# The last segment's keys and values are computed with the tokens moving, and the attention steps get another order

## The chip, the cores and the metric

The kernel runs on one core of one Trainium2 chip. The metric is the device time of one execution in microseconds (us). Three runs of the kernel before took 2739.06, 2739.63 and 2742.57 us; their median is 2739.63 us.

## The reference, cut to what matters

One transformer block on 2048 tokens of width 1024: a modulated layer norm, attention with a memory over 32 heads of 32, an output projection, a second modulated norm, and a gated feed-forward network. The tokens are four segments of 512. The part that the change touches:

```
h = layernorm(x) * (1 + ca) + sa
q, k, v = h @ wq, h @ wk, h @ wv            # 32 heads of 32
for s in range(4):                          # segments of 512 tokens
    logits = qs @ ks.T * scale + mask       # mask as in the reference
    a_dot  = softmax(logits) @ vs
    a_mem  = (phi(qs) @ M) / (phi(qs) @ z + 1e-6)
    o      = g * a_mem + (1 - g) * a_dot    # g = sigmoid(beta)
    M, z   = M + phi(ks).T @ vs, z + sum(phi(ks))
x = x + ga * (o @ wo)
```

After the last segment M and z are not needed any more, so of its keys only ks in the logits is used.

## The kernel before, in words

Everything is float32. Products run on TensorE (PE) in its fp32r form. For accuracy an operand is split into a high and a low part, and a product is three matmuls: high by high, low by high, high by low.

**Steps.** Eight groups of four heads times four segments make 32 steps. Steps 0 to 15 take segments 0 and 1 of each group in turn, steps 16 to 31 segments 2 and 3; so the last segment is that of the odd steps from 17 on. The loop in `attention` runs n from 0 to 32. In its round n it computes the scores of step n, the values of step n - 1 and the projections of step n + 1, all interleaved. The projections for the last segment are therefore made in the even rounds 16 to 30.

**What sets the order.** No scheduler works here: the instructions of all five engines stand in the order in which the code issues them, and that is written by hand in the table ORDER, a string of short names for every round. The names that matter:

- K0 to K7 (K in round 0): the products of keys and values in eight pieces, `keys` in `project_in` (L384). The hidden tokens (128 of them) are the operand held in the array, the weights of keys and values (256 columns) move past. A piece is 12 matmuls. Q0 to Q3: the queries' product, six matmuls a piece (L390), weights held and 512 tokens moving.
- o0, o1: ScalarE (ACT) copies the keys and VectorE (DVE) the values out of PSUM (L401, L402). kt: TensorE turns the keys (four transposes, L418), ACT and DVE split them (L421, L422). dk, dq: DMAs that spread keys and queries over the rows of `ks` and `qs`.
- qo, ea, eb: split and exponent of the queries (L447 to L461).
- S0 to S3: the scores of 128 queries by 128 to 512 keys, four heads (L541), their row maxima on DVE (L543) and exponents with row sums on ACT (L545). tr: the logarithm of the row sums (L550). tm, tq: maxima and logarithms are joined, turned and written into `qs` on DVE (L554 to L565). T needs them.
- T0 to T3: the scores once more, transposed (L629), exponent on ACT (L631), the triangle cut on GpSimd (POOL, L632). P0, P2: their product with the values (L641). rm, yt, zs: the memory's part is added and the result stored.
- A, mz, nu, dn: the memory's state (L580) and its numerators and denominators.
- G, C and D, l, L and m: load of the next group's weights, their high part on ACT (L369), their low part on POOL (L375). wl, wd: columns of the modulation. x: the hidden tokens of segments 2 and 3 are loaded and split. In rounds 31 and 32 all K and Q stand for pieces of the output projection (L708) instead, six matmuls each; every piece also runs a step of side work, such as `load_late`, which multiplies the second half of `wo` by the gate (DVE, L685) and splits it (ACT L189, POOL L194).

**Buffers.** Two PSUM banks take the products of K and Q in turn, five take S, T and all small results, one the output of P. A bank is used again when its readers are done.

After the attention come the rest of the output projection and the feed-forward network, two stages with 4704 and 2352 matmuls (L1133, L1347), which the change leaves as they are.

Of the kernel before, what the change touches and what calls it, by code (L numbers as in the profile page):

```python
# [12 lines left out]
F32R = mybir.dt.float32r  # L13
AF = mybir.ActivationFunctionType
# [14 lines left out]
NSEG = 4  # L29
# [7 lines left out]
def block_kernel(ctx: ExitStack, tc: tile.TileContext, x, c, wmod, wq, wkv, wo, beta, wg, wu, wd, out):  # L37
    nc = tc.nc
    f32 = lambda ap: ap.bitcast(F32)
# [53 lines left out]
    def mm_ps(name):  # L93
        return psum.tile([P, L], F32, name=name, tag="mm", bufs=2)
# [4 lines left out]
    def s_ps(name):  # L99
        return small[0].tile([P, L], F32, name=name, tag="s", bufs=small[2])  # L100
# [9 lines left out]
    def t2(name, tag, bufs=1, dt=F32, shape=(P, L)):  # L110
        return (p1 if tag in ("qs", "row") else pa).tile(list(shape), dt, name=name, tag=tag, bufs=bufs)
# [241 lines left out]
    ks_t = []  # L353
# [32 lines left out]
    def q_mm(ps, g, s, kt, **kw):  # L386
        hi, lo = hT[s][kt]
        w = W[g][0].rearrange("p h (k m) -> p h k m", m=P)[:, :, kt]
        for a, b in ((0, hi), (0, lo), (1, hi)):
            nc.tensor.matmul(ps, w[:, a], b, start=(kt == 0 and a == 0 and b is hi), stop=(kt == KT - 1 and a == 1), **kw)  # L390
# [421 lines left out]
    def feed_forward():  # L812
# [562 lines left out]
        for m in range(NCH):  # L1375
# [32 lines left out]
    steps = [(hf, g, s) for hf in range(2) for g in range(G) for s in (2 * hf, 2 * hf + 1)]  # L1408
    ORDER = {
        (0,):  # L1410
            "N K K N G1 K N N G2 K G0 K S0 S1 C1 S2 K S3 C2 K l1 l2 A tr tm tq L1 K K L2 K",
        (1,):
            "T0 K0 mz K1 T1 A P0 T2 ns K2 K3 nc D0 T3 n0 K4 nd n1 o0 K5 S0 m0 Q0 S1 K6 S2 m1 Q1 S3 Q2 Q3 nu dn ne nl K7 "
            "qo tr P2 o1 rm ea tm tq kt dq dk yt eb zs ek",
        (2, 4, 6, 8):
            "wd Q0 G2 Q1 Q2 T0 ns Q3 T1 P0 nc T2 A T3 qo n0 K0 nd S0 K1 ea C2 S1 G1 eb dq K2 S2 K3 C1 n1 l2 K4 l1 S3 K5 "
            "P2 nl o0 L2 tr tm K6 tq rm L1 K7 yt G0 wl o1 kt dk ek zs ne",
        (3, 5, 7):
            "mz D0 K0 K1 m0 T0 K2 T1 K3 ns m1 P0 nc T2 wl o0 n0 Q0 S0 K4 A S1 Q1 S2 K5 S3 n1 Q2 K6 nl Q3 tr wd T3 tm qo "
# [12 lines left out]
            "K5 C1 S3 x ea A wd l1 L1 G0 eb K6 dq x K7 P2 o1 tr rm tm kt tq yt ek x dk x x zs x x",
        (15,):
            "D0 K0 m0 K1 m1 K2 T0 K3 o0 T1 K4 S0 Q0 S1 Q1 S2 mz Q2 x S3 A tr Q3 P0 x T2 tm K5 T3 nu K6 K7 wl tq qo ea P2 "
            "o1 x eb wl rm dn x wd kt dq yt dk zs ek",
        (16,):
            "K0 G1 wd T0 mz x Q0 T1 A P0 x T2 Q1 T3 G2 Q2 S0 K1 S1 Q3 S2 K2 K3 o0 qo ea C2 C1 S3 tr P2 l2 G0 rm l1 eb K4 "
            "K5 K6 tm dq K7 o1 nu tq yt L2 dn kt L1 ek dk zs",
        (17,):
            "K0 D0 m0 K1 m1 K2 T0 K3 T1 P0 T2 o0 Q0 T3 wl S0 S1 Q1 S2 Q2 Q3 qo S3 K4 K5 ea K6 K7 P2 mz eb o1 tr rm tm kt "  # L1440
            "tq dq yt dk nu dn ek zs",
        (18, 20, 22, 24, 26, 28):
            "K0 G2 K1 K2 T0 mz K3 G1 o0 T1 K4 S0 C2 Q0 S1 P0 S2 Q1 T2 G0 Q2 Q3 wd T3 qo C1 K5 S3 K6 l1 A K7 P2 o1 tr dq "
            "tm kt L1 rm yt wl ek tq l2 nu dn dk ea eb L2 zs",
        (19, 21, 23, 25, 27):
            "K0 D0 K1 K2 m0 T0 K3 o0 wl T1 K4 S0 Q0 S1 P0 mz m1 wd wd T2 wl Q1 T3 S2 Q2 Q3 qo K5 S3 K6 dq K7 P2 o1 tr tm "
            "kt tq rm yt nu dk dn ek zs ea eb",
        (29,):
            "K0 D0 K1 m0 wd K2 T0 K3 o0 ga T1 K4 S0 K5 wo mz S1 P0 S2 m1 Q0 ga S3 Q1 tr wo tm Q2 T2 Q3 T3 K6 P2 K7 qo ea "
            "nu tq rm dq o1 yt dn kt eb dk ek wl zs",  # L1450
        (30,):
            "mz K0 ga x x T0 K1 T1 wp wp K2 K3 wl wl P0 o0 S0 K4 S1 Q0 S2 Q1 x wo x S3 x wo x Q2 K5 tr x K6 T2 K7 T3 wp "
            "Q3 tm tq nu qo P2 x ea o1 dq eb rm yt dn A x kt dk x x x x zs ek",
# [119 lines left out]
    def attention(nseg1):  # L1573
# [145 lines left out]
```

## Time and profile before

| what | value |
|---|---|
| median of three runs | 2739.63 us |
| the profiled execution's own time | 2743.34 us |
| its span, first to last instruction | 2741.5 us |
| granted TensorE clock, mean | 0.998 |
| busy: PE / DVE / ACT / POOL | 2706.3 / 1545.3 / 1191.4 / 843.6 us |
| attention, rounds 0 to 32 | up to about 980 us |
| scores' first matmuls of rounds 18 and 30 begin at | 573.10 and 903.50 us |

The views are read as follows. A row of a group has its line, engine and operation, what is written and read, the shape and the count; then its busy time, the mean length of one in ns, and the idle time of the engine just before it with what ended it. Matmuls overlap in their pipeline, so the mean length of one is longer than the distance from one to the next; that is the busy time of a long unbroken run by its count. A row of waits has the waiting instruction, what ended the wait, the sum in us, how often, and the longest. A row of a stretch has its borders and length, then for each engine busy time and count, the granted TensorE clock, the share of the DMA engines and GB/s. A row of the timeline has start, length, engine, line, operation, and in brackets the idle time before it.

### The profile page before, as it was taken

The page shows a single profiled execution, that of the slowest core. Times are in us where ns is not written, and L with a number is a line of the kernel's source. Part 1 is how long each engine was busy: PE and PEld are TensorE (multiplying, and loading weights), DVE is VectorE, ACT ScalarE, POOL GpSimd, SP SyncE. Part 2 cuts the span into 40 slices and gives each one's busy share as a digit, 9 for nine tenths or more (in the row PEclk, how much of TensorE's full clock was granted, in tenths as well). Part 3 has the DMA queues.
Part 4 walks back from the last instruction along what each step waited for, and adds up shares of the span by engine and source line. Part 5 has one row for each costly group of instructions (what it writes and reads, how often), then busy time and mean ns, then how long its engine had stood idle before and what let it go on. Part 6 is the DMA issues. An engine that isn't in the chain of part 4 may idle for free.

```text
span 2741.5 us, 42690 instructions
## 1 busy us (share of the span) xinstructions
PE 2706.3 (99%) x14620; PEld 2270.8 (83%) x14620; DVE 1545.3 (56%) x3455; ACT 1191.4 (43%) x2811; POOL 843.6 (31%) x1446
## 2 busy tenths in 40 slices
PE   7999999999999999999999999999999999999999
PEld 6888888888888878888888888888888888888887
DVE  7676666667667735555555555343443254575456
ACT  6777777676767624333323233111111033233323
POOL 4333234423333534254455452443531000000000
PEclk9999999999999999999999999999999999999999
DMA  7455444444443558778898778999998687795563
GB/s 261 110 153 142 121 142 143 131 112 139 119 133 104 166 197 294 250 287 328 307 356 308 266 278 278 358 364 356 359 358 313 218 316 254 263 305 200 184 206 125
DMA packets 244889, 637.76 MB, mean 233 GB/s; under 512 B 24768, under 2 KB 49344, under 8 KB 244672
## 3 DMA queue, kind: packets, MB, share of 16 engines
q1 hardware_dynamic: 244672, 635.03, 68.5%
q8 instruction: 116, 1.90, 0.3%
q14 instruction: 101, 0.83, 0.1%
HBM read 372.79 MB, written 211.81 MB: 213 GB/s over the span
## 4 chain that ended last, share of the span: by engine, by line
PE 91%; DVE 3%; DMA 2%; ACT 1%; issue 1%; POOL 1%; SPq 0%; DVEq 0%; ACTq 0%; POOLq 0%
PE f L1133 38%; PE y L1347 19%; PE kv L384 11%; PE q L390 6%; PE y L708 5%; PE S L541 3%; PE T L629 3%; PE O L641 3%; DVE qs L565 1%; ACT sj L545 1%; PE M L580 1%; PE kv L513 1%; PE num L597 1%; PE tpb L267 0%; PE kT L418 0%
## 5 line engine op out<-in xcount | busy, mean ns | idle before, releaser
L1133 PE MATMUL f<-A,B 128*128 128x512 f32 x4704 | 1072.9, 390 | 0.1
L1133 PEld LDWEIGHTS f<-A,B 128*128 128x128 f32 x4704 | 881.6, 188 | 184.4 <-issue 1.0
L1347 PE MATMUL y<-B,L 128*128 128x512 f32 x2352 | 533.3, 389 | 0.0
L1347 PEld LDWEIGHTS y<-B,L 128*128 128x128 f32 x2352 | 441.6, 188 | 91.5
L545 ACT ACTIVATE sj<-sj,mm 128x384 f32<-128x384 f32 (+3 forms) x512 | 281.8, 556 | 59.3 <-DVE mm L543 57.8
L543 DVE CUSTOM_DVE_ANT_0 sj<-S,mask 128x384 f32<-128x384 f32 (+3 forms) x512 | 226.0, 488 | 90.4 <-PE S L541 65.7
L632 POOL TENSOR_SCALAR_AFFINE_SELECT pt<-pt 128x128 f32<-128x128 f32 x512 | 161.8, 335 | 366.2 <-ACT pt L631 359.1
L631 ACT ACTIVATE pt<-T 128x256 f32<-128x256 f32 (+3 forms) x512 | 181.9, 441 | 141.1 <-PE T L629 136.8
L847 ACT ACTIVATE L<-X 128x512 fp32r<-128x512 f32 x168 | 105.8, 629 | 259.1 <-PE y L1347 166.9
L384 PE MATMUL kv<-w,hhh 128*128 128x256 f32 x1024 | 200.0, 285 | 0.0
L849 DVE TENSOR_TENSOR L<-X,L 128x512 fp32r<-128x512 f32 x168 | 116.0, 691 | 147.1 <-ACT L L847 147.1
L1167 ACT ACTIVATE g<-g 128x512 f32<-128x512 f32 x56 | 35.4, 631 | 369.4 <-DVE g L1166 369.4
L384 PE MATMUL kv<-w,hha 128*128 128x256 f32 x896 | 178.1, 286 | 0.3 <-DVE vx L402 0.3
L1072 POOL TENSOR_TENSOR rw<-rw,gbb 128x256 f32<-128x256 f32 x112 | 92.2, 858 | 249.3 <-DMA rw<-wd 184.8
L384 PEld LDWEIGHTS kv<-w,hhh 128*128 128x128 f32 x1024 | 164.8, 190 | 1.5 <-issue 0.4
L375 POOL TENSOR_TENSOR w<-r,w 128x256 fp32r<-128x256 f32 x180 | 131.5, 760 | 98.6 <-ACT w L369 98.6
L384 PEld LDWEIGHTS kv<-w,hha 128*128 128x128 f32 x896 | 145.7, 191 | 2.4 <-issue 0.8
L384 PE MATMUL kv<-w,hlh 128*128 128x256 f32 x512 | 144.6, 282 | 0.0
L708 PE MATMUL y<-wo,hho 128*128 128x512 f32 x384 | 127.3, 396 | 0.8 <-DVE xr L712 0.6
L384 PE MATMUL kv<-w,hla 128*128 128x256 f32 x448 | 126.8, 283 | 0.0
L1154 ACT ACTIVATE g<-f 128x512 f32<-128x512 f32 x56 | 33.5, 598 | 204.4 <-PE f L1133 204.4
L629 PE MATMUL T<-qs,ks 128*128 128x256 f32 (+3 forms) x512 | 108.0, 330 | 6.4 <-DVE qs L565 4.4
(240 smaller groups left out, 4093.0 us busy)
## 6 DMA issues: line engine op xcount, KB each, us to landing
bc_d<-B SPq DMA_DIRECT2D x189, 512.0 KB, 5.2
B<-bc_d SPq DMA_DIRECT2D x189, 512.0 KB, 5.6
B<-wc_d SPq DMA_DIRECT2D x112, 512.0 KB, 4.1
hid_d<-g SPq DMA_DIRECT2D x56, 512.0 KB, 4.3
wc_d<-T SPq DMA_DIRECT2D x56, 512.0 KB, 7.2
X<-hid_d SPq DMA_DIRECT2D x112, 256.0 KB, 4.7
wr<-gd_d SPq DMA_DIRECT2D x84, 256.0 KB, 4.1
qs<-qh SPq DMA_DIRECT2D x64, 256.0 KB, 3.6
```

The lines of the kernel that those rows point to most:

```text
L375: nc.gpsimd.tensor_sub(w[:, 1, c], r[:, c], f32(w[:, 0, c]))
L384: nc.tensor.matmul(ps, b[:, sl], w[:, a], start=(kt == 0 and a == 0 and b is hi), stop=(kt == KT - 1 and a == 1), **kw)
L390: nc.tensor.matmul(ps, w[:, a], b, start=(kt == 0 and a == 0 and b is hi), stop=(kt == KT - 1 and a == 1), **kw)
L543: nc.vector.tensor_tensor_reduce(out=sj[:, :nv], in0=ps[:, :nv], in1=mask[:, L - nv:], scale=-1.0, scalar=3.4e38, op0=ALU.add, op1=ALU.min ...
L545: nc.scalar.activation(sj[:, :nv], sj[:, :nv], AF.Exp, bias=mm[:, j, i:i + 1], scale=-1.0, accum_out=ll[:, i, j:j + 1])
L629: nc.tensor.matmul(ps[:, :nn], ks[:, j, kc * P:(kc + 1) * P], qs[:, j, L - nn:], start=True, stop=True)
L631: nc.scalar.activation(pt, ps[:, nn - n:nn], AF.Exp)
L632: nc.gpsimd.affine_select(pt[:, :P], pt[:, :P], pattern=[[1, P]], compare_op=ALU.is_ge, fill=0.0, base=0, channel_multiplier=-1)
L708: nc.tensor.matmul(ps, b[:, i * P:(i + 1) * P], w[:, a, g % 2], start=(g == 0 and a == 0 and b is hi), stop=(g == G - 1 and a == 1))
L849: eng.tensor_sub(lo[:, k], src[:, k], f32(hi)[:, k])
L1133: nc.tensor.matmul(ps, B[m, i][:, a, kt * P:(kt + 1) * P], A[p, i, kt][b], start=(start and kt == 0 and a == 0 and b == 0), stop=(kt == 3 ...
L1347: nc.tensor.matmul(banks[t], ops[k][:, y, t * P:(t + 1) * P], B[slots[k]][:, x], start=(i not in (2, 4, 3) and j == 0 and x == 0 and y == ...
```

## The change

For the last segment `project_last` takes the place of `project_in`. Its K0 to K3 make the keys and K4 to K7 the values, with the weights held and 512 tokens moving: six matmuls of 512 columns in a piece instead of twelve of 256. Keys come out turned already, so o0 splits them at once (ACT and DVE); values come out with tokens in the columns, o1 copies them (ACT), and a new name vt turns them (four transposes, one DVE copy) in place of kt.

```diff
+    def side_mm(ps, g, s, half, kts):
+        for kt in kts:
+            hi, lo = hT[s][kt]
+            w = W[g][1 + kt // 4].rearrange("p h (k m) -> p h k m", m=2 * P)[:, :, kt % 4, half * P:(half + 1) * P]
+            for a, b in ((0, hi), (0, lo), (1, hi)):
+                nc.tensor.matmul(ps, w[:, a], b, start=(kt == 0 and a == 0 and b is hi), stop=(kt == KT - 1 and a == 1))
+
+    def project_last(u, n, g, s):
...
+        def columns(i):
+            half, q = divmod(i, 4)
+            if q == 0:
+                ps[half] = mm_ps(f"{'kv'[half]}T{nm}")
+            side_mm(ps[half], g, s, half, (2 * q, 2 * q + 1))
...
+        def keys():
...
+            nc.scalar.activation(t["h"], ps[0], AF.Copy)
+            nc.vector.tensor_sub(t["l"], ps[0], f32(t["h"]))
+
+        def vals():
+            t["v"] = t2("vt" + nm, "kn")
+            nc.scalar.activation(t["v"], ps[1], AF.Copy)
+
+        def turned():
...
+            vs = s_ps("vv" + nm)
+            for i in range(4):
+                nc.tensor.transpose(vs[:, i * P:(i + 1) * P], t["v"][:, i * P:(i + 1) * P], ident)
+            nc.vector.tensor_copy(vx[:, :, :P], vs.rearrange("p (t m) -> p t m", m=P))
...
-                project_in(u, n + 1, *steps[n + 1][1:])
+                (project_last if steps[n + 1][2] == NSEG - 1 else project_in)(u, n + 1, *steps[n + 1][1:])
```

All strings of ORDER are new. Two of them, of the last round and of the even rounds from 18 to 28:

```diff
         (18, 20, 22, 24, 26, 28):
-            "K0 G2 K1 K2 T0 mz K3 G1 o0 T1 K4 S0 C2 Q0 S1 P0 S2 Q1 T2 G0 Q2 Q3 wd T3 qo C1 K5 S3 K6 l1 A K7 P2 o1 tr dq "
-            "tm kt L1 rm yt wl ek tq l2 nu dn dk ea eb L2 zs",
+            "G2 K0 wl K1 T0 wd K2 T1 K3 o0 P0 mz T2 A G1 T3 G0 S0 K4 S1 C1 P2 S2 dk K5 Q0 S3 tr Q1 Q2 C2 tm l1 Q3 K6 tq "
+            "qo rm L1 K7 l2 nu o1 yt dn ea eb dq L2 zs vt",
         (32,):
-            "K0 Q0 K1 K2 T0 Q1 T1 K3 Q2 P0 T2 Q3 T3 K4 K5 K6 P2 rm yt zs K7",
+            "Q0 K0 K1 K2 T0 K3 T1 Q1 P0 T2 Q2 T3 K4 P2 K5 rm K6 K7 yt zs Q3",
```

Three places at which the engines' rows differ. Changed lines have numbers higher by 55 from L541 on (L545 is L600, L550 is L605, L629 is L684, L631 is L686).

*PE, first product for the last segment (round 16).* `kv_3` is the PSUM tile of keys and values, `kT_3` that of the turned keys, `hhh` and `hlh` are high and low parts of the hidden tokens, `w_1` the weights. Before:

```order
L418 MATMUL kT_2_7157<-ident,kn_2_6777 128x128 x4
L384 MATMUL kv_3_0_7181<-w_1_0_6635,hhh_1_0_6751 128x256
L384 MATMUL kv_3_0_7181<-w_1_0_6635,hlh_1_0_6752 128x256
L384 MATMUL kv_3_0_7181<-w_1_0_6635,hhh_1_0_6751 128x256
L384 MATMUL kv_3_0_7181<-w_1_0_6635,hhh_1_1_6758 128x256
...
L629 MATMUL T_1_00_7197<-qs_1_6617,ks_117 128x512
```

Now:

```order
L418 MATMUL kT_2_7158<-ident,kn_2_6764 128x128 x4
L503 MATMUL kT_3_7190<-hhh_1_0_6758,w_1_0_6546 128x512
L503 MATMUL kT_3_7190<-hlh_1_0_6759,w_1_0_6546 128x512
L503 MATMUL kT_3_7190<-hhh_1_0_6758,w_1_0_6546 128x512
L503 MATMUL kT_3_7190<-hhh_1_1_6826,w_1_0_6546 128x512
...
L684 MATMUL T_1_00_7203<-qs_1_6535,ks_117 128x512
```

Between the same neighbours twelve matmuls of 256 columns have become six of 512 (the rows left out go on in the same way), held and moving operand have changed places, and the tile holds keys alone.

*ACT and PE, from round 0 to round 1.* `sj` are exponents of scores, `w_0_1` high parts of the next group's weights, `ln` the logarithm of the row sums, `kn` copies of keys. ACT before, and now:

```order
L545 ACTIVATE sj_0_23_896,ll_0_806<-sj_0_23_896,mm_0_805 128x512
L545 ACTIVATE sj_0_33_901,ll_0_806<-sj_0_33_901,mm_0_805 128x512
L369 ACTIVATE w_0_1_904<-r_0_1_771 128x1024
L550 ACTIVATE ln_0_932<-ll_0_806 128x16
L401 ACTIVATE kn_1_690<-kv_1_0_693 128x256
L401 ACTIVATE kn_1_690<-kv_1_1_694 128x256
L421 ACTIVATE kh_1_975<-kT_1_970 128x512
L447 ACTIVATE qh_1_979<-q_1_695 128x512
```

```order
L600 ACTIVATE sj_0_23_892,ll_0_802<-sj_0_23_892,mm_0_801 128x512
L600 ACTIVATE sj_0_33_897,ll_0_802<-sj_0_33_897,mm_0_801 128x512
L605 ACTIVATE ln_0_900<-ll_0_802 128x16
L369 ACTIVATE w_0_1_902<-r_0_1_823 128x1024
L369 ACTIVATE w_0_1_928<-r_0_1_769 128x1024
L401 ACTIVATE kn_1_690<-kv_1_0_693 128x256
L401 ACTIVATE kn_1_690<-kv_1_1_694 128x256
L421 ACTIVATE kh_1_973<-kT_1_968 128x512
```

The logarithm has moved ahead of the split of the weights, and both splits (the first stood between the second and third row of scores) now follow it. PE at the same border; `kT` are the turned keys of step 1, `kv_0` the first products of round 1, `T` the transposed scores. Before, and now:

```order
L418 MATMUL kT_1_970<-ident,kn_1_690 128x128 x4
L629 MATMUL T_0_00_1000<-qs_0_601,ks_116 128x512
...
L629 MATMUL T_0_30_1015<-qs_0_601,ks_116 128x512
L384 MATMUL kv_0_0_1023<-w_0_1_847,hha_0_263 128x256
L384 MATMUL kv_0_0_1023<-w_0_1_847,hla_0_264 128x256
```

```order
L418 MATMUL kT_1_968<-ident,kn_1_690 128x128 x4
L384 MATMUL kv_0_0_1005<-w_0_1_928,hha_0_263 128x256
...
L384 MATMUL kv_0_0_1005<-w_0_1_902,hha_7_534 128x256
L684 MATMUL T_0_00_1065<-qs_0_601,ks_116 128x512
...
L684 MATMUL T_0_30_1080<-qs_0_601,ks_116 128x512
L267 MATMUL tpa_0_1085<-ident,na_676 128x128 x4
```

T0 came right behind the turned keys; now four pieces, K0 to K3 with 48 matmuls (rows left out), stand between them.

*ACT, end of round 32.* `pt` are the exponents of T2 (`pt_3_32` is its last) and T3 (`pt_3_03` on), `wo` and `ks` the second half of the output weights, whose split waits for the gate's product. Before, and now:

```order
L631 ACTIVATE pt_3_32_13704<-T_3_32_13702 128x256
L189 ACTIVATE wo_1_13715<-ro_0_13676 128x1024
L631 ACTIVATE pt_3_03_13724<-T_3_03_13722 128x128
L631 ACTIVATE pt_3_13_13729<-T_3_13_13727 128x128
L631 ACTIVATE pt_3_23_13734<-T_3_23_13732 128x128
L631 ACTIVATE pt_3_33_13739<-T_3_33_13737 128x128
L189 ACTIVATE wo_2_13750<-ro_1_13713 128x1024
L189 ACTIVATE ks_116<-ro_2_13748 128x1024
L189 ACTIVATE ks_117<-ro_3_13764 128x1024
```

```order
L686 ACTIVATE pt_3_32_13293<-T_3_32_13291 128x256
L686 ACTIVATE pt_3_03_13309<-T_3_03_13307 128x128
L686 ACTIVATE pt_3_13_13314<-T_3_13_13312 128x128
L686 ACTIVATE pt_3_23_13319<-T_3_23_13317 128x128
L686 ACTIVATE pt_3_33_13324<-T_3_33_13322 128x128
L189 ACTIVATE wo_1_13335<-ro_0_13305 128x1024
L189 ACTIVATE wo_2_13358<-ro_1_13333 128x1024
```

The split of `wo_1` stood ahead of T3's exponents, now it stands behind them. POOL, which follows the same order, has T3's four cuts ahead of the low parts of `wo_1` likewise.

More of the change, by code (lines that the diff above doesn't have):

```diff
@@ L495, in project_in, with queries @@
         after_kv(u, n, s, nm, lambda: st)
+        after_q(u, n, s, nm, lambda: ps["q"])
+    def side_mm(ps, g, s, half, kts):
[5 more added lines that the diff above has]
+    def project_last(u, n, g, s):
+        nm = f"{g}_{s}"
+        ps, t = {}, {}
+        ks = ks_t[n % 2]
+        ST[n] = [None, ks, None, None]
+        def columns(i):
[3 more added lines that the diff above has]
+            side_mm(ps[half], g, s, half, (2 * q, 2 * q + 1))
+        def queries(i):
+            if i == 0:
+                ps["q"] = mm_ps("q" + nm)
+            for kt in (2 * i, 2 * i + 1):
+                q_mm(ps["q"], g, s, kt)
+        def keys():
+            t["h"] = t2("kh" + nm, "sp", bufs=4, dt=F32R)
+            t["l"] = t2("kl" + nm, "sp", bufs=4, dt=F32R)
+            nc.scalar.activation(t["h"], ps[0], AF.Copy)
[4 more added lines that the diff above has]
+        def turned():
+            vx = t2("vx" + nm, "vx", bufs=3, shape=(P, 4, P + 2))
+            nc.gpsimd.memset(vx[:, :, P:], 1.0)
+            ST[n][2] = vx
+            vs = s_ps("vv" + nm)
+            for i in range(4):
+                nc.tensor.transpose(vs[:, i * P:(i + 1) * P], t["v"][:, i * P:(i + 1) * P], ident)
+            nc.vector.tensor_copy(vx[:, :, :P], vs.rearrange("p (t m) -> p t m", m=P))
+        for i in range(8):
+            u[f"K{i}"] = lambda i=i: columns(i)
+        for i in range(4):
+            u[f"Q{i}"] = lambda i=i: queries(i)
+        u["o0"] = keys
+        u["o1"] = vals
+        u["vt"] = turned
+        u["dk"] = lambda: spread(ks, ((0, t["h"]), (1, t["h"]), (2, t["l"])))
         after_q(u, n, s, nm, lambda: ps["q"])
@@ L1438, in block_kernel @@
[L1438 removed]
+            "G1 K0 K1 T0 K2 T1 P0 T2 mz K3 o0 T3 K4 G2 S0 K5 S1 P2 C2 C1 rm S2 Q0 K6 S3 Q1 l1 tr Q2 yt nu dn K7 Q3 o1 L1 "
+            "l2 G0 tm qo ea dk A L2 dq tq vt eb zs wl",
         (17,):
[L1440 to L1441 removed]
+            "K0 D0 m0 K1 K2 T0 m1 K3 o0 T1 K4 S0 Q0 S1 Q1 S2 K5 S3 P0 T2 tr mz Q2 Q3 T3 K6 K7 tm qo P2 tq o1 ea rm kt yt "
@@ L1447, in block_kernel @@
-            "kt tq rm yt nu dk dn ek zs ea eb",
+            "K0 wd K1 T0 K2 mz T1 K3 wl D0 S0 wl o0 K4 m0 S1 m1 P0 S2 Q0 S3 Q1 wd tr K5 Q2 T2 Q3 tm T3 K6 K7 qo ea tq P2 "
+            "o1 kt rm yt nu dn dq dk eb zs ek",
         (29,):
-            "K0 D0 K1 m0 wd K2 T0 K3 o0 ga T1 K4 S0 K5 wo mz S1 P0 S2 m1 Q0 ga S3 Q1 tr wo tm Q2 T2 Q3 T3 K6 P2 K7 qo ea "
-            "nu tq rm dq o1 yt dn kt eb dk ek wl zs",
+            "K0 wo wd mz K1 D0 T0 m0 K2 T1 K3 ga o0 S0 Q0 S1 P0 S2 m1 Q1 S3 Q2 K4 T2 Q3 tr K5 tm T3 K6 P2 K7 nu tq qo rm "
```

44 lines of the change are left out of this document (22 added, 22 removed).

## The prediction

> **What bounds the kernel now.** I began with the page's head, then read the stretches, the waits of PE, and last the places of the longest waits.
>
> ```profile
> span 2741.5 us, 42690 instructions
> PE 2706.3 (99%) x14620; PEld 2270.8 (83%) x14620; DVE 1545.3 (56%) x3455; ACT 1191.4 (43%) x2811; POOL 843.6 (31%) x1446
> ```
>
> PE is busy for 2706.3 of 2741.5 us: it bounds every stage, and only two things can move the end by much, the work on PE and its 35.2 us of idle time. By stretches (us, then busy time of PE, PEld, DVE, ACT, POOL, granted clock):
>
> ```profile
> 0.00:100.00 100.00, 78.36 (x497) 67.91 (x498) 67.96 (x183) 65.99 (x127) 41.16 (x78) 0.95 0.58 197
> 100.00:300.00 200.00, 200.00 (x1460) 173.16 (x1461) 137.61 (x473) 154.74 (x445) 62.93 (x164) 1.00 0.53 145
> 300.00:520.00 220.00, 216.09 (x1588) 185.88 (x1586) 151.45 (x471) 156.02 (x454) 91.25 (x200) 1.00 0.49 143
> 520.00:850.00 330.00, 328.98 (x2467) 288.50 (x2469) 223.76 (x765) 232.42 (x687) 109.59 (x268) 1.00 0.44 122
> 850.00:990.00 140.00, 135.90 (x859) 110.76 (x852) 89.95 (x250) 87.13 (x241) 70.39 (x134) 0.99 0.47 142
> 990.00:2741.00 1751.00, 1746.94 (x7760) 1444.58 (x7758) 874.55 (x1316) 495.06 (x863) 468.31 (x604) 1.00 0.80 284
> ```
>
> Of the attention, rounds 1 to 9 (100 to 300) and 18 to 28 (520 to 850) leave 0 and 1.0 us; the rest of the idle time lies at the start, in rounds 10 to 16 (3.9) and at the end of the attention (4.1). Behind 990 PE runs without a gap in work that isn't changed, so a microsecond won before is a microsecond of the end. The waits of PE:
>
> ```profile
> PE scp L143 <- DVE scdg L137: 11.1, 1, 11.1
> PE T L629 <- DVE qs L565: 4.4, 1, 4.4
> PE tpa L328 <- ACT x L1527: 3.8, 1, 3.8
> PE O L641 <- POOL pt L632: 3.6, 1, 3.6
> PE M L580 <- DVE pk L432: 1.6, 3, 0.7
> PE T L629 <- DVE ry L608: 1.2, 6, 0.2
> PE q L390 <- DVE vx L402: 1.1, 1, 1.1
> ```
>
> The first and third belong to the opening, which keeps its order. What the new order can touch is 4.4 + 3.6 + 1.6 + 1.2 + 1.1 = 11.9 us, and what hangs on the two long ones.
>
> **The products.** A long run of the old form, a piece of the queries, which have the new one's shape already, and the longest run of that shape:
>
> ```profile
> 443.65:447.95 4.30, 4.27 (x36) 4.27 (x35) 1.00 0.76 183
> ...
> 433.90:435.33 1.43, 1.43 (x6) 0.99 (x6) 1.00 0.00 0
> ...
> L1133 PE MATMUL f<-A,B 128*128 128x512 f32 x4704 | 1072.9, 390 | 0.1
> ```
>
> A matmul of 256 columns costs 4.27 / 36 = 0.119 us, one of 512 columns 1072.9 / 4704 = 0.228. So the long form is hardly cheaper per column: a step's 96 short ones take 11.4 us, its 48 long ones 10.9. That is 0.5 us in each of eight steps, 4 us. At the dear end, 1.43 / 6 = 0.238, the 48 take 11.4 us too and nothing is won. I take 3.5, since the pieces stand among the shapes of attention and the long run does not.
>
> [...]
>
> On the other engines the counts stay: four transposes then and now, ACT copies 512 + 512 columns instead of 256 + 256 + 512, DVE likewise. They cost nothing while covered by PE, and DVE and ACT are busy for 68% and 70% of 520 to 850. If the cover is gone, see the second rival.
>
> **Round 0 to round 1.** Now T0 stands first in round 1 and waits for tq:
>
> ```profile
> 69.78 1.05 ACT L369 ACTIVATE w<-r 128x1024 fp32r<-128x1024 f32 x1
> ...
> 75.96 1.04 ACT L369 ACTIVATE w<-r 128x1024 fp32r<-128x1024 f32 x1
> 76.91 0.20 ACT L550 ACTIVATE ln<-ll 128x16 f32<-128x16 f32 x1
> 77.08 4.32 POOL L375 TENSOR_TENSOR w<-r,w 128x256 fp32r<-128x256 f32 x6 [4.74 <-ACT w L369]
> 80.13 2.36 DVE L565 TENSOR_SCALAR qs<-tt,seli 32x512 fp32r<-32x512 f32 x4
> 82.52 0.76 DVE L402 COPY vx<-kv 128x256 f32<-128x256 f32 x2
> 82.55 2.07 PE L629 MATMUL T<-qs,ks 128*128 128x512 f32 x4 [4.42 <-DVE qs L565]
> 87.96 0.86 PE L629 MATMUL T<-qs,ks 128*128 128x384 f32 x4
> 82.55:86.00 3.45, 3.45 (x12) 3.06 (x13) 3.38 (x7) 2.06 (x4) 1.58 (x5) 0.51 0.24 79
> ```
>
> Two splits of weights on ACT stand ahead of the logarithm, and after the wait PE runs for 3.45 us at a clock of 0.51, so the place costs 4.4 + 1.7 = 6.1 us. In the new order both splits follow the logarithm, which comes about 2 us earlier (75.0); tq ends near 79 to 80. K0 needs a PSUM bank that the DVE copies behind tq (82.52 now) free, so near 79.5 to 80.5; late next is POOL: all four halves of the weights' low parts, eight instructions of 4.32 / 6 = 0.72 us from about 76.2, end at 82.0, and the last ones are K1's. K0 and K1 are then done by 82.2, where now T0, K0 and K1 are done at 87.96; T0 is 0.9 us of that. It leaves 87.96 - 82.2 - 0.9 = 4.9 us. Behind T2 and T3, which now follow each other, S0 has to wait for banks until ACT has passed seven exponents, about 0.7 us. I take 4, between 0 (the wait comes back at K0, with the slow clock) and 6.1.
>
> **End of round 32.** P2 waits for POOL's last cuts:
>
> ```profile
> 967.48 0.56 PE L629 MATMUL T<-qs,ks 128*128 128x128 f32 x4
> 968.53 1.23 DVE L685 TENSOR_TENSOR ro<-ro,gab 128x1024 f32<-128x1024 f32 x1 [5.23 <-DMA ro<-wo]
> 969.79 1.06 ACT L189 ACTIVATE wo<-ro 128x1024 fp32r<-128x1024 f32 x1 [2.58 <-DVE ro L685]
> 970.76 0.76 ACT L631 ACTIVATE pt<-T 128x128 f32<-128x128 f32 x4
> 970.94 5.09 POOL L194 TENSOR_TENSOR wo<-ro,wo 128x256 fp32r<-128x256 f32 x4 [3.37 <-ACT wo L189]
> 975.98 1.02 POOL L632 TENSOR_SCALAR_AFFINE_SELECT pt<-pt 128x128 f32<-128x128 f32 x4
> 976.33 1.37 PE L641 MATMUL O<-pt,vx 128*32 128x128 f32 x8 [3.57 <-POOL pt L632]
> 976.30:980.20 3.90, 3.87 (x16) 2.88 (x17) 0.69 (x1) 0.69 (x1) 3.90 (x8) 0.56 0.20 67
> ```
>
> T3 was on PE at 967.48, but its exponents stand behind a split that waits through DVE for a DMA, and its cuts behind 5.09 us of POOL. In the new order T3 comes one piece of the projection earlier (seven pieces before it, not eight), the split is the eighth piece's, and exponents and cuts go first. They end some 0.76 + 1.02 + 0.5 = 2.3 us after T3; K4 (six matmuls of 0.228) covers 1.4 and the first half of P2, which needs T2 alone, some of the rest. So 3.6 + 0.44 x 3.9 = 5.3 us go and 0.5 comes back: 4.8, ends 0 (another split holds the cuts) and 5.3. The work behind the split (the second half of `wo`) is first read a block of the projection later.
>
> [...]
>
> **Rounds 10 to 16 and the short waits.** T0 and A move back in rounds 11 and 13, so the 1.6 us go; in round 15 fewer loads of hidden tokens stand on DVE ahead of o0, so the 1.1 goes. Against it round 14 has T0, T1, P0 and T2 in a row, where banks and cuts hold PE for about 0.7. Net 2, ends 0 and 2.7. The six waits of 0.2 for `ry` go since K0 and K1 still stand ahead of T0 and dn comes at its old distance: 1, ends 0 and 1.2.
>
> **New waits.** C1 and C2 move behind S2 in rounds 2 to 8 and again to the end of the scores in 18 to 28. ACT then reaches the last exponents about 2 us later, and T0 of round 3 is left a margin of about 1 us. No row shows such a wait; by the nearest, 0.2 to 0.7 us each in 14 rounds, it is 0 to 8. I take 1, near the low end, since rounds with the same sequence show 0 in 200 us.
>
> **Sum.** 3.5 + 4 + 4.8 + 2 + 1 - 1 = 14.3 us, or 0.5%. The profiled execution took 2743.34 us, 0.14% above the median of 2739.63; less 14.3 it is 2729.0, and from the median 2725.3. I forecast 2725.
>
> **Rivals.** First, only the shape counts: new waits eat what the order wins, and the gain is the 3.5 us, 2736. For it speaks that 100 to 300 and 520 to 850 have next to nothing to win, against it that the two long waits have a plain cause in the rows.
>
> Second, slower: ACT becomes late in the last segment's rounds. From S0 to the copy of the values ACT has
>
> ```profile
> L545 ACT ACTIVATE sj<-sj,mm 128x512 f32<-128x512 f32 x40 | 28.4, 712 | 9.6 <-DVE mm L543 9.6
> L545 ACT ACTIVATE sj<-sj,mm 128x384 f32<-128x384 f32 x40 | 24.1, 606 | 1.9 <-DVE mm L543 1.6
> L545 ACT ACTIVATE sj<-sj,mm 128x256 f32<-128x256 f32 x40 | 19.8, 495 | 2.4 <-DVE mm L543 2.4
> L369 ACT ACTIVATE w<-r 128x1024 fp32r<-128x1024 f32 x15 | 16.0, 1065 | 0.0
> L545 ACT ACTIVATE sj<-sj,mm 128x128 f32<-128x128 f32 x40 | 15.6, 391 | 5.2 <-DVE mm L543 5.2
> ```
>
> 4 x (0.712 + 0.606 + 0.495 + 0.391) + 2 x 1.065 = 10.9 us and about 2 of small ones; PE has eight pieces of 1.4 and four scores, some 14. Vt waits for that copy, and behind vt the next round's K0. The margin is about 1 us; each microsecond of ACT beyond it costs 8 over the eight rounds. The end is later than before from a lag of 1 + 14.3 / 8 = 2.8 us a round; at 3.5 it is 2745. Against it: ACT is idle before S0 and can't carry a lag over.
>
> Third, all waits go and none is new: 4 + 6.1 + 5.3 + 2.7 + 1.2 = 19.3 us, and a few more of stretched matmuls at the borders of S and T that the list of waits leaves out: 2716.
>
> **Chances.** Forecast 0.70 (2718 to 2733), all gone 0.14, shape alone 0.10, slower 0.06. The range 2713 to 2735 takes in the third and the edge of the first. What a measurement can tell from no change is 0.2%, 5.5 us: faster is below 2734.1. Faster 0.84, same 0.10, slower 0.06.
>
> **What would show it.** In the profile after, the waits of PE have no T for qs over 1.5 us and no O for pt over 1; the two stretches at half clock are gone; a run of the new products stands at 0.228 to 0.238 us each; from S0 of round 18 to S0 of round 30, 330.4 us now, it is 3 to 5 less. Wrong it would be through a new row in that list, above all of vt for ACT, of K for DVE or POOL in rounds 1, 3 and 17, or of P2 for POOL in round 31.

## The result, and the profile after

| what | before | after |
|---|---|---|
| median time | 2740.25 us | 2723.47 us |
| ratio, with its 95% interval | | 0.994, 0.9926 to 0.9955 |
| span of the profiled execution | 2741.5 us | 2724.7 us |
| last product of the attention begins at (Y of round 32) | 978.32 us | 963.83 us |
| first and last product of the feed-forward's gate begin at | 1127.90, 2204.13 us | 1111.71, 2187.34 us |

The change takes 16.8 us off, in the medians and between the two spans; 2725 was forecast. What is won by the end of the output projection (16.2 us) stays. The head of the page after:

```profile
span 2724.7 us, 41937 instructions
PE 2696.7 (99%) x14236; PEld 2251.2 (83%) x14236; DVE 1538.4 (56%) x3447; ACT 1192.3 (44%) x2803; POOL 851.4 (31%) x1446
```

PE has 384 matmuls fewer (8 x 48). Its idle time is 28.0 us, 7.2 less than before, and its busy time 9.6 less. The stretches, with the columns of before, and PE's waits, longest first (the first three belong to the opening):

```profile
300.00:515.00 215.00, 214.46 (x1552) 183.73 (x1550) 145.02 (x459) 152.52 (x437) 89.98 (x195) 1.00 0.48 139
515.00:837.00 322.00, 322.00 (x2148) 271.07 (x2150) 223.22 (x746) 230.62 (x675) 116.70 (x272) 1.00 0.43 124
837.00:975.00 138.00, 136.61 (x819) 109.43 (x812) 94.03 (x261) 89.03 (x248) 71.75 (x135) 1.00 0.47 147
```

```profile
PE scp L143 <- DVE scdg L137: 11.1, 1, 11.1
PE tpa L328 <- ACT x L1582: 3.8, 1, 3.8
PE kv L568 <- ACT hha L341: 2.4, 1, 2.4
PE kv L384 <- DVE vx L402: 2.3, 1, 2.3
PE tpa L267 <- ACT na L246: 1.2, 1, 1.2
PE T L684 <- DVE ry L663: 1.1, 1, 1.1
```

T for qs and O for pt, 4.4 and 3.6 us before, are down to 0.4 and 0.2; M for pk (1.6) and q for vx (1.1) are gone, and no wait for the values' new turn (vt) has come. Four rows are new or larger: the 2.4 of the opening (0.9 before), the 2.3 of round 1's K0, the 1.2 behind it, and T's 1.1 for ry. The six waits of 0.2 for ry are gone; this one is new and stands in T0 of round 31.

The list of waits doesn't hold all of it. For an account by place I gave each matmul a price by its shape, the same in both kernels (0.109 us for 128 columns, 0.119 for 256, 0.175 for 384, 0.228 for 512, O's 0.028 to 0.076), and call the rest of the time lost. Between the last S products of the rounds named, in us:

| stretch | lost before | lost after | won | the sum said |
|---|---|---|---|---|
| opening and round 0 | 27.6 | 29.8 | -2.3 | 0 |
| rounds 1 and 2 | 10.4 | 9.5 | 0.9 | 4 |
| rounds 3 to 9 | 12.8 | 9.3 | 3.6 | new waits, -1 |
| rounds 10 to 16 | 18.6 | 17.8 | 0.8 | 2 |
| rounds 17 to 31 | 27.8 | 24.5 | 3.3 | waits for ry, 1 |
| round 32, output projection | 7.8 | 1.8 | 6.0 | 4.8 |
| feed-forward (below nothing, as its long runs go at 0.227) | -7.1 | -7.7 | 0.6 | 0 |
| the products, 8 x (96 x 0.119 - 48 x 0.228) | | | 3.8 | 3.5 |
| sum | | | 16.8 | 14.3 |

### The profile page after: what moved, and what is told of

It is laid out like the page before. It is cut to its first block, busy times and chain, and to the rows that moved or that the text cites. A ratio compares the mean times of both kernels' runs of the same rounds, so it can differ in the third digit from the quotient of the medians.

```text
span 2724.7 us, 41937 instructions
## 1 busy us (share of the span) xinstructions
PE 2696.7 (99%) x14236; PEld 2251.2 (83%) x14236; DVE 1538.4 (56%) x3447; ACT 1192.3 (44%) x2803; POOL 851.4 (31%) x1446
## 4 chain that ended last, share of the span: by engine, by line
PE 96%; DVE 1%; ACT 1%; DMA 1%; issue 0%; POOL 0%; SPq 0%; ACTq 0%; DVEq 0%; POOLq 0%
PE f L1188 39%; PE y L1402 20%; PE kv L384 9%; PE y L763 6%; PE q L390 6%; PE S L596 3%; PE T L684 3%; PE O L696 3%; PE kT L503 2%; PE vT L503 2%; PE num L652 1%; PE M L635 1%; PE kv L568 1%; ACT sj L600 1%; PE tpb L267 1%; PE kT L418 0%
## 5 line engine op out<-in xcount | busy, mean ns | idle before, releaser
L600 ACT ACTIVATE sj<-sj,mm 128x384 f32<-128x384 f32 (+3 forms) x512 | 281.1, 552 | 40.1 <-DVE mm L598 39.6
L686 ACT ACTIVATE pt<-T 128x256 f32<-128x256 f32 (+3 forms) x512 | 182.3, 444 | 132.5 <-PE T L684 125.8
L1199 ACT ACTIVATE c<-f 128x512 f32<-128x512 f32 x56 | 33.4, 597 | 173.9 <-PE f L1188 173.9
L684 PE MATMUL T<-qs,ks 128*128 128x256 f32 (+3 forms) x512 | 105.6, 327 | 1.8 <-DVE ry L663 1.1
L596 PE MATMUL S<-ks,qs 96*128 96x384 f32 (+3 forms) x512 | 106.9, 329 | 0.2
L684 PEld LDWEIGHTS T<-qs,ks 128*128 128x128 f32 x512 | 80.9, 189 | 25.0 <-issue 12.1
```

Of the source, the lines that this page charges most:

```text
L596: nc.tensor.matmul(ps[:, :nk], qs[:96, j, i * P:(i + 1) * P], ks[:96, j, :nk], start=True, stop=True)
L600: nc.scalar.activation(sj[:, :nv], sj[:, :nv], AF.Exp, bias=mm[:, j, i:i + 1], scale=-1.0, accum_out=ll[:, i, j:j + 1])
L684: nc.tensor.matmul(ps[:, :nn], ks[:, j, kc * P:(kc + 1) * P], qs[:, j, L - nn:], start=True, stop=True)
L686: nc.scalar.activation(pt, ps[:, nn - n:nn], AF.Exp)
```

## The experiments

### The two halves of the change apart

*shape_alone*: the new products in the order of before.

```diff
 # in the strings of rounds 16, 18 to 28 and 30 of before
-kt ... ek
+vt
```

> The order of before with the new products for the last segment (vt stands where kt stood). Theory, by the change's trace: a short matmul goes at 0.1215 us between its like and a long one at 0.233, so 96 x 0.1215 - 48 x 0.233 = 0.48 us a step, 3.8 us in eight steps: some 2736 where before has 2740, the six steps between the scores of rounds 17 and 28 2.9 us shorter than the 303.3 us of before, and both stretches at half clock still there. [...] Second rival: ACT gets late with the longer copies in the old order, and new waits of PE for ACT eat the gain: 2740 or more.

Median 2739.5 against 2742.26 us, ratio 0.9991 (0.9983 to 1.0). By the trace the last S of round 28 comes 300.25 us behind that of round 17 (303.29 before), the end of the attention 3.7 us earlier from the end of round 0. The theory holds: 2.5 us by the ratio of the times, 3.7 by the trace, with one wait of 0.6 us for ry as the new cost. The times alone, 0 to 4.7, would leave room for no gain at all; the trace doesn't, since the five profiles of other kernels with the old products in this order have 303.1 to 303.4 us for those rounds. The price of the long form can be read in the change's trace, in two runs of 12 matmuls in round 22, of the values and of the keys:

```profile
690.02:692.74 2.72, 2.72 (x13) 2.25 (x12) 2.61 (x8) 1.97 (x4) 2.22 (x3) 1.00 0.23 86
667.11:669.96 2.85, 2.85 (x15) 2.34 (x14) 2.75 (x10) 0.64 (x2) 0.00 (x0) 1.00 0.80 197
```

From the first matmul to the one behind the twelfth it is 2.72 and 2.85 us, 0.227 and 0.238 each (the counts take in the ends of matmuls before them).

*order_alone*: the change's order with the old products.

```diff
-(project_last if steps[n + 1][2] == NSEG - 1 else project_in)(...)
+project_in(...)
 # rounds 18 to 28
-... P2 S2 dk K5 ... o1 yt dn ea eb dq L2 zs vt
+... P2 S2 K5 ... o1 yt kt dn ea dk eb dq L2 zs
```

> The change's order with the old products for the last segment (kt and dk behind o1 in rounds 16 to 30, since keys have to be turned there). Theory: what the order wins does not hang on the products, so the gain is that of the whole change less 3.8 us, 13 to 15 us: 2726 to 2728 where before has 2740 and the change 2723.5. Rival: the order needs the new products (their keys come out turned, without four transposes ahead of the spread), and with the old ones PE waits in rounds 18 to 30: the gain is under 9 us.

Median 2757.32 us, ratio 1.0058 (1.0045 to 1.007): 15 us slower than before. My theory fell, the rival holds. Its largest waits behind round 13:

```profile
PE S L541 <- DMA qs<-ql: 13.4, 8, 2.3
PE kv L384 <- DVE vx L402: 2.8, 6, 0.5
PE kv L384 <- DVE hhh L220: 1.7, 1, 1.7
```

The scores of the next round wait for the queries' DMAs. On SP's queue these stand behind the keys', which can't start before the keys are turned at the end of the round:

```profile
646.49 1.20 SPq L407 DMA_DIRECT2D ks<-kh  x2
647.78 0.56 SPq L407 DMA_DIRECT2D ks<-kl  x1
648.39 1.26 SPq L407 DMA_DIRECT2D qs<-qh  x2
649.70 0.61 SPq L407 DMA_DIRECT2D qs<-ql  x1
```

The last is issued at 649.70; S begins at 656.24.

*queries_first*: the same with the queries' DMAs ahead of the keys'.

```diff
-tq qo rm L1 K7 l2 nu o1 yt kt dn ea dk eb dq L2 zs
+tq qo dq rm L1 K7 l2 nu o1 yt kt dn ea dk eb L2 zs
```

> The change's order with the old products, as in the run before, but the queries' DMAs (dq) go out right behind qo, ahead of the keys' (dk). Theory: the waits of S for qs (13.4 us) and the slow clock behind some of them go; what is left is K0 for vx (5.0): 2733 to 2740, between the run with dk first (2757) and the change. Rival: the old products' keys are late in any case, and S waits for ks in place of qs: over 2750.

Median 2735.16 us, ratio 0.9974 (0.9963 to 0.9985). The 13.4 us are gone; the other two rows are still there, with the same numbers. So of the change's 17 to 19 us (here and in a second comparison, below) the order gives some 8 without the products, with dq moved besides, and the products 2.5 without the order; the other 6 to 8 need both. The traces say the same: from the last S of round 0 to the last matmul of the output projection the change takes 18.5 us less than before, this kernel 6.4 and *shape_alone* 4.3. One reason is a row that this kernel has six times behind round 13 and the change never: K0 waits for vx, 2.8 us in all. With the old products a bank of PSUM is free when DVE has copied the values, and DVE has four writes of qs ahead of that copy; with the new ones ACT's copy frees it. What makes up the rest isn't settled.

*late_spread*: the change with the keys' DMAs named late.

```diff
-... P2 S2 dk K5 ... ea eb dq L2 zs vt
+... P2 S2 K5 ... ea eb dk dq L2 zs vt
```

> The change with one name moved in its even rounds from 16 on: dk, the three DMAs that spread the keys, stands at the end of the round directly ahead of dq, not behind S2. Theory: what the new products give is less their 0.48 us a step than that the keys are ready and spread early, so that the queries' three DMAs at the end of the round land in time. With six DMAs there the first scores of rounds 17 to 31 wait for the queries as in the run with the old products (S for qs 13.4 us, eight times): 8 to 14 us slower than the change, 2732 to 2738. Rival: the DMAs have room there; then the time is the change's, within 1 us, and the 15 us of that run came from the work of turning the keys late.

Median 2722.42 us, ratio 0.9927 (0.9915 to 0.994), the change's time; the rival holds. SP's rows show why the edit did nothing:

```profile
618.75 1.20 SPq L407 DMA_DIRECT2D ks<-kh  x2
620.04 0.55 SPq L407 DMA_DIRECT2D ks<-kl  x1
631.58 1.19 SPq L407 DMA_DIRECT2D qs<-qh  x2
```

Here dk goes out 12.8 us ahead of dq, though the string names one right behind the other, and in the change's trace, where the string has them far apart, it is 12.8 us too (624.12 and 636.95). What differs in order_alone is when the keys are ready.

### The two long waits

*start_alone* and *end_alone*: before with the strings of rounds 0 and 1, and with that of round 32, of the change.

```diff
 # start_alone: the strings of rounds 0 and 1 of the change
 # end_alone, round 32
-K0 Q0 K1 K2 T0 Q1 T1 K3 Q2 P0 T2 Q3 T3 K4 K5 K6 P2 rm yt zs K7
+Q0 K0 K1 K2 T0 K3 T1 Q1 P0 T2 Q2 T3 K4 P2 K5 rm K6 K7 yt zs Q3
```

> Before, with the strings of rounds 0 and 1 of the change alone. The prediction gave this place 4 us. Theory now, by the change's trace: the wait of T0 (4.4 us) and the slow clock behind it (1.7) go, but the products of round 1 wait 2.3 us for the copies of values that stand on DVE behind four writes of qs, the hidden tokens' transposes wait 1.2 us for ACT, and cuts and banks hold PE for about 1.3 more: the end is 0.5 to 1.5 us earlier than before, no slow stretch near 82. Rival: the 4 us come here and were lost in round 0 or 2 of the change; then the end is 4 us earlier.

> Before, with the string of round 32 of the change alone, which puts T3 one piece of the output projection earlier, ahead of the split. The prediction gave this place 4.8 us. Theory now, by the change's trace: 3.6 us of waiting and the slow clock behind it go wholly, 1.7 + 0.6 of small waits, so 6 us, and no slow stretch near 977. Rival: 4.8, with half a microsecond of waiting left at P2. Third: the wait alone goes (3.6) and the clock still falls.

end_alone: 2736.04 us, ratio 0.9979 (0.997 to 0.9988), 5.8 us by that ratio; by the trace it loses 6.4 us less from the last S of round 31 to the end of the output projection. The theory holds: POOL makes the four cuts of T3 (the first row below), and the split begins 2.7 us behind them; P2 waits 0.2 us, and no slow stretch follows (the granted clock is 1.00 from 960 to 976).

```profile
966.78 1.02 POOL L632 TENSOR_SCALAR_AFFINE_SELECT pt<-pt 128x128 f32<-128x128 f32 x4 [0.55 <-ACT pt L631]
970.53 2.07 POOL L194 TENSOR_TENSOR wo<-ro,wo 128x256 fp32r<-128x256 f32 x2 [2.73 <-ACT wo L189]
```

start_alone: 2746.35 us, ratio 1.0014 (1.0005 to 1.0023), 4 us slower. Round 1 alone loses 0.5 us less than before, within the theory's range, though a slow stretch stands at 80 to 84 (the granted clock is 0.95 over 68 to 102), which the theory ruled out. In its profile, which is 1.6 us longer than that of before, the loss comes from a place that the edit doesn't touch: the output projection waits for a load (y for xr, 3.2 us at 1110) and loses 3.5 us more. That this makes the 4 us of the other executions too is likely, not shown, and why the load is late here and neither before nor in the change isn't settled.

K0's wait in the change, in PE's and DVE's rows:

```profile
82.79 0.39 PE L384 MATMUL kv<-w,hha 128*128 128x256 f32 x1 [2.25 <-DVE vx L402]
...
77.64 0.19 DVE L609 TENSOR_TENSOR mm<-mm,ln 128x16 f32<-128x16 f32 x1 [1.24 <-ACT ln L605]
...
79.18 3.09 DVE L620 TENSOR_SCALAR qs<-tt,seli 32x512 fp32r<-32x512 f32 x4
82.31 0.76 DVE L402 COPY vx<-kv 128x256 f32<-128x256 f32 x2
```

The four writes of qs take 3.09 us where they took 2.36 before. POOL's splits run beside them: the first write took 0.49 us, the other three 0.95 each, and the splits went from 0.74 to 0.91. Before, the splits ended during the second write, and the last two took 0.48 each.

### Rounds 2 to 9

*a_between* and *a_k_between*: before with A, and with A and K0, moved as the change has them.

```diff
 # rounds 2, 4, 6, 8 of before; first a_between, then a_k_between
-T1 P0 nc T2 A T3 qo n0 K0 nd S0
+T1 nc A P0 T2 T3 qo n0 K0 nd S0
+T1 nc A P0 T2 K0 T3 qo n0 nd S0
```

> Before with A (the memory's product, eight matmuls of 130 columns) moved from behind T2 to between T1 and P0 in rounds 2, 4, 6 and 8, as the change's string of these rounds has it among other moves. Theory: P0's second half waited there for POOL's four cuts of T1 one by one, 0.27 to 0.35 us for each of three matmuls, which the list of waits does not show; the rows go from 107 to some 50 ns, 0.8 us a round, 3 us in all. Rival: the gain of rounds 2 to 9 in the change (3.9 us) came from other moves of these strings, the later K0 above all; then under 1 us.

> Before with A between T1 and P0 and, besides, K0 between T2 and T3 in rounds 2, 4, 6 and 8. Theory: with A alone the waits of P0 for cuts went (107 to 49 ns a matmul) but T3's banks became late in their place (94 to 196 ns); with a piece of products there too, 0.8 us a round go, 3 us in all, most of the 3.9 that the change wins in rounds 2 to 9. Rival: the wait goes on to S0, which now follows T3 without K0; then it stays at 0.2 a round.

Both take the time of before: ratios 0.9999 (0.999 to 1.0008) and 1.0001 (0.9992 to 1.001). By the trace a round loses 0.2 and 0.1 us less, so both theories fell. The rows of 160 to 272 us of before, a_between and the change, in this order, show how:

```profile
L641 PE MATMUL O<-pt,vx 128*32 128x384 f32 x32 | 4.9, 490 | 0.0
L629 PE MATMUL T<-qs,ks 128*128 128x128 f32 x16 | 2.5, 277 | 0.0
```

```profile
L629 PE MATMUL T<-qs,ks 128*128 128x128 f32 x16 | 3.3, 281 | 0.2
L641 PE MATMUL O<-pt,vx 128*32 128x384 f32 x32 | 3.3, 486 | 0.0
```

```profile
L696 PE MATMUL O<-pt,vx 128*32 128x384 f32 x32 | 3.3, 486 | 0.0
L684 PE MATMUL T<-qs,ks 128*128 128x128 f32 x16 | 2.2, 262 | 0.0
```

32 equal matmuls are busy for 4.9 us before and 3.3 in the change; the 1.6 us are waits for POOL's cuts, hidden in busy time since one matmul's modelled end covers the next one's wait (in round 4 three of them last 0.27 to 0.35 us each, as the cuts end 0.25 to 0.38 us apart). a_between takes them out and T3 gets 0.8 us in their place; a_k_between takes that out too, and then S waits:

```profile
PE S L541 <- ACT hta L275: 2.2, 4, 0.6
```

The wait is handed on along the line of banks. The change spreads T, P, K and n0 over the whole round and wins 3.6 us in rounds 3 to 9; which of its moves are needed isn't settled.

### A version that mends three places

*mended*: the change with these edits.

```diff
 # round 0
-S3 tr C2 A K G0 C1 tm K l2 tq l1 K L1 K L2
+S3 tr C1 A K G0 C2 tm K l1 K L1 K l2 tq L2
 # round 1
-D0 K0 K1 ns K2 nc K3 T0 n0 n1 mz A K4 T1 P0
+D0 K0 K1 ns K2 K3 T0 nc mz A K4 T1 n0 n1 P0
 # round 14
-T0 T1 P0 T2 x wd S0 x K0 x G2 G1 S1 wd Q3 T3 K1 ... S2 K2 K3 K4 S3 K5
+T0 K0 T1 Q3 P0 T2 x wd S0 x K1 x G2 G1 S1 wd T3 K2 ... S2 K3 K4 S3 K5
 # round 31
-Q0 K0 K1 K2 x T0 K mz wd S0 K3 K T1
+Q0 K0 K1 K2 x K T0 mz wd K3 S0 K T1
```

> The change with three places mended. Round 0: the copies of the values stand on DVE ahead of the writes of qs (tq last), POOL makes the low parts that K0 needs first; round 1: nc behind T0, and the transposes n0, n1 behind T1. Round 14: K0 between T0 and T1, Q3 between T1 and P0. Round 31: a piece of the output projection ahead of T0. Theory: the wait of K0 for vx (2.3 us), of the transposes for ACT (1.2), of T0 in round 31 for qs (1.9) and about 2 us of P0's waits for cuts in round 14 go: 5 to 7 us less than the change, 2717 to 2719. Rival: at the start POOL is what is late, and K0 waits for the low parts in place of the bank: then the start gives under 1 us and the whole 3 to 4.

Median 2721.89 us, ratio 0.9923 (0.9911 to 0.9936). By the trace the start gives 3.4 us (round 1 loses 4.2, not 7.7; K waits 0.3 us for POOL and the transposes don't wait) and round 31 0.4, less than the wait of T0 that was to go; round 14 gives nothing (4.54 against 4.58): P0's waits for cuts went, but T3 has 0.9 us of them for banks, and K waits 1.5 us for pq, the last reader of the queries' bank. From the last S of round 0 to the end of the output projection it takes 1034.4 us, the change 1037.9, 1037.8 in its second profile. The theory held at the start and fell in round 14. In the times the 3.5 us don't stand out: the interval of the ratio overlaps with the change's.

What the next theory takes for the cause in round 14, in mended's rows of POOL and DVE:

```profile
446.79 3.04 POOL L687 TENSOR_SCALAR_AFFINE_SELECT pt<-pt 128x128 f32<-128x128 f32 x4 [19.02 <-ACT pt L686]
```

```profile
446.74 1.22 DVE L172 CUSTOM_DVE_ANT_0 wm<-wm,scb 128x1024 f32<-128x1024 f32 x1
...
447.88 1.30 DVE L172 CUSTOM_DVE_ANT_0 wm<-wm,scb 128x1024 f32<-128x1024 f32 x1
```

*wd_later* and *mended2* move these DVE instructions behind S2, in the change and in mended; *change_again* is the change beside them.

```diff
 # round 13
-... dk eb ek wd
+... dk eb ek
 # round 14 (wd_later)
-T2 x wd S0 x K0 x G2 G1 S1 wd Q3 ... S2 K2 K3 K4 S3 K5 l2 x L2 l1 L1 K6
+T2 x S0 x K0 x G2 G1 S1 Q3 ... S2 wd K2 K3 K4 S3 K5 wd l2 x L2 l1 L1 wd K6
```

> The change with three of the names wd (a column of the modulation, DVE L172, 1.22 us of reading and writing SBUF) moved from the end of round 13 and the first half of round 14 to behind S2 of round 14. Theory: while that instruction runs POOL's cut stands still, 1.28 and 1.32 us where a cut takes 0.29, so P0 of round 14 waits for cuts; with wd away the round loses 2.0 to 2.9 us where it lost 4.6: 1.7 to 2.6 less than the change. Rival: it is the close sequence T0, T1, P0, T2 itself, since each cut waits for its exponent; then the round keeps its 4.5.

> The mended version with the three wd moved likewise. Theory: the start's 3.4 us and round 31's 0.4 stay, and round 14 falls from 4.5 to about 2.5: 5.5 to 6 us less than the change, 2717 to 2718. Rival: as for the run before, round 14 keeps its loss, and it is 3.5 us less.

> The change as it is, beside the two versions of it that follow: 2722 to 2724, as in its first runs.

change_again: 2723.86 us, ratio 0.9932 (0.992 to 0.9945). wd_later: 2738.39, 0.9983 (0.9975 to 0.9992); mended2: 2734.46, 0.997 (0.996 to 0.9981): both slower than what they start from by 13 to 15 us. Round 14 falls to 3.9 in wd_later, 0.7 of the 2 us that the theory gave, so the close sequence has the larger part, as the rival says: with cuts of 0.29 us T1 still waits 0.9 us for banks and P0 0.8 for cuts. In mended2 it stays at 4.5. Round 15 then loses 12 to 14 us more. Columns, weights and hidden tokens are loaded into the same four buffers (`raw_tile`); a column that waits for its wd holds one, and SP stands at the next load. The same two loads of weights (r<-wkv) and what SP waited for ahead of them, in the change and in wd_later, and PE's wait in the latter:

```profile
452.96 1.57 SPq L124 DMA_DIRECT2D r<-wkv  x2
...
SPq L124 <- DVE modT L172: 3.2, 1, 3.2
```

```profile
461.08 5.03 SPq L124 DMA_DIRECT2D r<-wkv  x2
...
SPq L124 <- DVE hlh L225: 9.7, 1, 9.7
```

```profile
PE kT L418 <- ACT kn L401: 6.4, 2, 5.9
```

In the change the buffer comes from a column (DVE L172), in wd_later only from the split of hidden tokens (DVE L225), 8 us later.

## Why the prediction was right, point by point

**The products, 3.5.** 3.8 at the account's prices; alone 2.5 by the times (0 to 4.7) and 3.7 by the trace. In the change's trace the long form stands at 0.227 to 0.238 and the short one at 0.119, as the steps took them.

**Round 0 to 1, 4.** 0.9: the term that failed. Up to K0 its steps held. Counted from the last S of round 0, which is 2.26 us later in the profile after, the logarithm begins at 75.1 on the clock of before (75.0 was worked out), the writes of qs end at 80.0 (79 to 80) and K0 begins at 80.5 (79.5 to 80.5); so the wait of 2.3 us ahead of K0 lies inside the steps. What failed is "K0 and K1 are then done by 82.2". That is about the end of POOL's low parts, which I put last in the chain; DVE's copies were last, and the 24 matmuls of K0 and K1 take 2.9 us behind them by the prediction's own price. They ended at 83.5, 1.3 us later than in the sum. Besides, the 1.2 us of n0 and 1.3 at P0 and T1 were in no term. The first of these is DVE's too, since ACT, which n0 waits for, stood idle for the statistics that DVE makes (mra):

```profile
89.68 1.24 ACT L246 ACTIVATE na<-na,mra,rsa 128x1024 f32<-128x1024 f32 x1 [6.07 <-DVE mra L244]
```

mended puts the copies first and the transposes later, and gets 3.4.

**End of round 32, 4.8.** 6.0; end_alone 5.8 by the times. The 0.5 us put down as coming back was 0.2, and the account's 6.0 holds small waits ahead of P2 besides.

**Rounds 10 to 16, 2.** 0.8. The waits for pk and vx went, as said, but T0, T1, P0 and T2 in a row cost round 14 1.6 us more than before, not 0.7.

**Waits for ry, 1, and new waits, -1.** 3.3 in rounds 17 to 31 and 3.6 in rounds 3 to 9. The six waits for ry went, against one of 1.1 in round 31, but they are the smaller part. The steps read "next to nothing to win" from the idle times of 100 to 300 and 520 to 850. That was wrong, since PE's busy time holds waits: O's 1.6 us above, and in rounds 18 to 28 T's first four matmuls, before and after:

```profile
L629 PE MATMUL T<-qs,ks 128*128 128x512 f32 x44 | 13.2, 403 | 1.0 <-DVE ry L608 1.0
```

```profile
L684 PE MATMUL T<-qs,ks 128*128 128x512 f32 x44 | 11.9, 391 | 0.0
```

1.3 us of busy time and 1.0 of waiting went. C1 and C2 behind the scores made no wait for the last exponents, and no row shows PE waiting for ACT behind round 1. So the net of these two terms, 0 in the sum, was 6.9 us: they were both mis-sized, for that one reason.

**What lay outside the sum.** The opening, whose order is the same, lost 2.3 us more in the profile after: a load of the modulation landed 1 us later, PE waited 2.4 us for what hung on it (0.9 before), and the window behind the wait, at 29.92, ran at 0.50 where before's clock is 1.00. In the change's second profile it lost 27.0 us, less than before's 27.6. So the sum came within 2.5 us of the result partly by luck, since its errors have both signs: too much for the start and rounds 10 to 16, too little for the end and for what busy time hides. The terms that carried it, the products and the end, 9.8 of the 16.8 us, are the two that the experiments confirm by themselves.

**The signs that it named.** The two waits are below their bounds, the new products stand at 0.227 to 0.238, and behind the opening no stretch is slow in the first profile; the second has one at 80.6. K for DVE in round 1 is among the rows named as signs of being wrong, and it did mark the term that failed. From S0 of round 18 to S0 of round 30 it takes 322.4 us, 8.0 less and not 3 to 5. This sign was badly set: the new order has P0, T2, T3 and A ahead of S0 in round 18, so the stretch holds 2.9 us less work. The other 5.1 are 2.8 for the products and 2.3 for waits.

## What to carry to other kernels

Where PE is 99% busy, the list of waits is not all there is to win: compare the busy time of equal groups of matmuls, in ns from one to the next, between stretches. When a row of instructions moves beside others, take its length from a place where the same engines run beside it (the four writes of qs took 2.36, 3.09 and 1.69 us). A form of product can be worth more than its own price if it makes a buffer free on another engine, or a result ready earlier on a queue (with the old products K0 waited 2.8 us for vx and S 13.4 for qs); ask that before costing its columns alone.

## What the runs showed of the hardware

**The slow clock comes by windows.** In the traces of before and of the change the slow stretches begin at multiples of 3.413 us from one another (before: 38.14, 82.51 and 976.80, the last two 13 and 275 windows behind the first; the change: 29.92 and 40.16, 3 windows apart). The same wait of K0 in two executions of the change, first and second profile, in such windows (PE's busy time is the first number behind the length, the clock the third from the end):

```profile
81.12:84.53 3.41, 1.74 (x14) 1.75 (x15) 3.35 (x7) 2.49 (x5) 3.41 (x6) 1.00 0.61 151
84.53:87.94 3.41, 3.41 (x31) 3.41 (x30) 3.34 (x6) 0.00 (x0) 0.48 (x2) 1.00 0.92 227
```

```profile
77.19:80.60 3.41, 1.16 (x9) 0.85 (x9) 3.35 (x6) 2.88 (x6) 3.41 (x5) 1.00 0.31 96
80.60:84.01 3.41, 3.41 (x19) 3.41 (x18) 3.34 (x6) 0.21 (x1) 1.59 (x4) 0.50 0.88 205
```

In the first the wait of 2.3 us falls across two windows (PE is busy for 2.37 us of the one before, 77.71 to 81.12) and nothing follows; in the second it lies in one, and the next window runs at half. Other windows at full clock, by PE's busy time in them:

| PE busy, us | window begins at | clock of the next window |
|---|---|---|
| 0.00 | before, 79.10 | 0.50 |
| 0.47 | before, 973.39 | 0.50 |
| 1.29 | the change, 26.51 | 0.50 |
| 1.72 | order_alone, 884.89 | 0.50 |
| 2.02 | the change, 917.39 | 1.00 |
| 2.14 | before, 75.68 | 1.00 |

So half a window of idle time was followed by a slow one in order_alone (1.72 busy) and not in the change (1.74). Idle time was not needed for it in the opening: before's window at 34.73 and the change's at 36.75, where PE is busy for 3.41 us with 25 and 23 matmuls of one column among others, were followed by two windows at 0.50 each. A wait of 4.4 us would leave one of its two windows at most 1.2 us of work however the border falls ((2 x 3.41 - 4.4) / 2), less than the 1.29 above; that it costs the clock in any position is my estimate from these rows. One of 2.3 us did so in one execution and not in the other. Nor did the slow window cost 1.7 us here: by the account both profiles lose the same in round 1 (7.68 and 7.66), since n0's wait for ACT (1.2) is not there where PE comes later.

**A cut took four times as long beside one kind of DVE instruction.** A cut of POOL takes 0.29 us, so also the first three of round 14 in wd_later, whose L172 come later. In mended's rows above, with DVE's L172 beside them, the four took 3.04 us; in the change's trace, where the four stand the same way, the two that began at 451.77 and 453.04, beside L172, took 1.31 and 1.27. Why is not shown. The writes of qs and POOL's splits slow each other as well. In mended, where POOL's splits are done before the writes begin, the writes of round 1 take 1.69 us and not 3.09:

```profile
77.06 5.78 POOL L375 TENSOR_TENSOR w<-r,w 128x256 fp32r<-128x256 f32 x8 [14.93 <-ACT w L369]
84.05 1.69 DVE L620 TENSOR_SCALAR qs<-tt,seli 32x512 fp32r<-32x512 f32 x4
```

That isn't a full stop of one of the two. Side by side one write and one split take 0.87 us from start to start, less than the 0.41 and 0.69 that they need alone come to (1.10).
